# Moving the newest adds, an addition and the expert layers within a fused attention and mixture-of-depths kernel

## The chip, the cores and the metric

The kernel runs on one core of one Trainium2 chip. The metric is the device time of one execution in microseconds (us). Before the change the median of three runs was 548.92 us (548.64 to 553.21).

The engines are named as in the profile: PE is TensorE (matmuls), PEld its weight loads, DVE is VectorE, ACT is ScalarE, POOL is GpSimd, and SP is the queue from which most DMAs are issued. Each works through its own instructions in the order in which the program emits them, and waits where another engine has to deliver first.

## The reference

Eight batches of attention, 12 heads, 448 tokens, head size 64, with normalised queries and keys. Its output, brought to `x[8, 448, 768]`, goes into a mixture of depths: a gate scores each token, the best 128 of a batch pass through two layers (768 to 1024 to 768), and the rest are copied.

```python
def rmsnorm(x, g):
    rms = np.sqrt(np.mean(x * x, axis=-1, keepdims=True) + 1e-06)
    return x / rms * g
q_n, k_n = (rmsnorm(q, g_q), rmsnorm(k, g_k))
scores = scale * np.matmul(q_n, k_n.transpose(0, 1, 3, 2))
attn = np.exp(scores - max); attn = attn / (sum + 1e-09)
out = np.matmul(attn, v)            # -> x (B, S, 768)
...
scores = np.einsum('bsd,d->bs', x, w_gate)
out = x.copy()
for b in range(B):
    top_idx = np.argpartition(-scores[b], capacity)[:capacity]   # 128
    xe = x[b, top_idx]
    ye = np.maximum(xe @ w1, 0.0) @ w2
    g = 1.0 / (1.0 + np.exp(-scores[b, top_idx]))
    out[b, top_idx] = x[b, top_idx] + g[:, None] * ye
```

(The line with `max` and `sum` is shortened from the original's.)

## The kernel before, in words

All the work is in the function `fast`. The 96 heads are taken in 24 **groups** of four (three groups to a batch). A group has seven **units**, each of them 64 of the 448 keys for its four heads, so there are 168 units.

For a unit, `scores` (L276) makes scores with the keys on the partitions, and ScalarE their exponents `p` (L285), scaled by the keys' norms. `values` (L302) multiplies `p` with the values into two PSUM banks that collect over the seven units. `add_probs` (L315) adds the unit's `p` into `sum` on VectorE; the first unit of a group needs no add. After a group's last unit come the steps that `finish` queues as **tasks**: `sum_keys` (den, L337) lets TensorE sum `sum` over the keys; `invert_sums` (denT, L355, then rden, L357) transposes that and takes the reciprocal; `to_tokens` (x_ps, L369, then x, L371) transposes 128 columns of the output and multiplies with rden, twice per group; `last_tokens` is the second of them and puts `gate` (L395, four products) into the slots. With the batch's last group `spread` follows (L408 to L416), and as a task `ranks_of`: row_ps (L424), its copy score_rows (L428), `count` (cmp, L438), `annotate`, `select` (L465, POOL scatters the chosen rows to a DRAM tile) and `load_selected` (SP loads them back as xe).

`mixture` runs the layers on the 128 rows. It is a generator that is advanced piece by piece: six transposes of xe (L499, the first three into the bank moe_ps, the others into the shared bank aux as xeT_ps) with two copies to xeT (L504); w1 in four pieces (L523) with the ReLU (hT, L532) after every second; w2 in four pieces (L542), each half followed by the gated addition on VectorE (L551); then POOL scatters the rows to the output (L560).

Queries are normalised ahead: `squares` (L191, ScalarE), `sum_squares` (ss: reduction L197 and 1e-6 L198 on VectorE, power rinv L201 on POOL), the norms' way through DRAM (`rows_out`, `rows_in`), and `scale_q` (qT, L235), due four units before the group's first scores.

The order of all this is written out by the loop at the end of `fast`, which goes through **sections** of four units (numbered from 0 to 41, two units being a half). In a section it emits:

- two units' scores, the values of the two units before, the adds of those; then the same for the second half;
- opening 0: one task that is due (tasks are taken from the front two of the list);
- for each half: the slots of its two units (`run`: squares, ss, loads, scale_q, gate, count), a piece of a mixture, and another opening.

A section in which a mixture has no piece is called light here, one with w1 or w2 full. PSUM has four banks for scores, two for values, one (aux) for the tasks and one (moe) for the mixture; `spare` lets a task use the latter where no mixture does. A bank is written again only after its reader is done, so a task's matmul can wait for the reader of the task before.

After the last scores there are no more sections to fill: the last values, tasks and mixtures follow each other. This is called the tail.

Of the kernel before, what the change touches and what calls it, by code (L numbers as in the profile page):

```python
# [11 lines left out]
I32 = mybir.dt.int32  # L12
# [14 lines left out]
def fast(  # L27
# [45 lines left out]
    const = ctx.enter_context(tc.tile_pool(name="const", bufs=1))  # L73
    load_pool = ctx.enter_context(tc.tile_pool(name="load", bufs=2))
    norm_pool = ctx.enter_context(tc.tile_pool(name="norm", bufs=2))
    p_pool = ctx.enter_context(tc.tile_pool(name="p", bufs=7))
    x_pool = ctx.enter_context(tc.tile_pool(name="x", bufs=2))
    moe_pool = ctx.enter_context(tc.tile_pool(name="moe", bufs=1))
    dram_pool = ctx.enter_context(
# [9 lines left out]

    def aux(shape, name):  # L90

        if spare[0]:
            return ps_moe.tile(shape, F32, tag="moe", name=name)
        return ps_aux.tile(shape, F32, tag="aux", name=name)
# [100 lines left out]
    def sum_squares(n, i, sq):  # L195
        ss = sss.pop((n, i))
        nc.vector.tensor_reduce(out=ss, in_=sq, axis=AX.X, op=OP.add)  # L197
        nc.vector.tensor_scalar_add(out=ss, in0=ss, scalar1=1e-6)  # L198
        rinv = norm_pool.tile([128, 2, NI], F32, name="rinv", bufs=8)
        flat = "p h i -> p (h i)"  # L200
        nc.gpsimd.tensor_tensor(  # L201
            out=rinv.rearrange(flat),
            in0=ss.rearrange(flat),
            in1=neg_half.to_broadcast([128, 2 * NI]),
            op=OP.pow,
        )
        rinvs[n, i] = rinv
# [31 lines left out]
    def scale_q_early(n):  # L239

        rinv = rinvs.pop((n, 0))
        for c in range(2):
            ps = ps_sc.tile([128, 512], F32, name="sc")
            r = slice(D * c, D * (c + 1))
            for i in range(NI):
                for hh in range(2):
                    nc.tensor.matmul(
                        out=ps[D * hh : D * (hh + 1), D * i : D * (i + 1)],
                        lhsT=rinv[r, hh, i : i + 1].to_broadcast([D, D]),
                        rhs=ident[r, r],  # L250
                        start=True,
                        stop=True,
                    )
            t = qTs[n][:, c].rearrange("d (p i) -> d p i", i=NI)
            nc.vector.scalar_tensor_tensor(
                out=t,
                in0=t,
                scalar=gg,
                in1=ps[:, 0:S].rearrange("d (i p) -> d p i", i=NI),
                op0=OP.mult,  # L260
                op1=OP.mult,
            )
# [4 lines left out]

    def scores(u):
        n, i = divmod(u, NI)
        scs = [ps_sc.tile([128, 512], F32, name="sc") for _ in range(2)]  # L270
        for c in range(2):
            for k0 in (0, 32):
                for hh in range(2):
                    r = slice(D * hh, D * (hh + 1))
                    o = D * c + k0
                    nc.tensor.matmul(  # L276
                        out=scs[hh][o : o + 32, 0:S],
                        lhsT=kTs[n][r, c, D * i + k0 : D * i + k0 + 32],
                        rhs=qTs[n][r, c, :],
                        start=True,  # L280
                        stop=True,
                    )
        p = p_pool.tile([128, 2, S], F32, name="p")
        for hh in range(2):
            nc.scalar.activation(  # L285
                out=p[:, hh],
                in_=scs[hh][:, 0:S],
                func=AF.Exp,
                scale=rinvs[n, 1][:, hh, i : i + 1],
            )  # L290
        probs[u] = p
# [194 lines left out]
    def mixture(b):  # L486

        n = CAP
        xe = xes.pop(b)
        xeT = moe_pool.tile([128, NDC, 128], F32, name="xeT")  # L490
        half = NDC // 2
        for a in range(2):
            if a == 0:
                ps = ps_moe.tile([128, 512], F32, tag="moe", name="moe_ps")
            else:
                ps = aux([128, 512], "xeT_ps")
            for i in range(half):
                dc = half * a + i
                nc.tensor.transpose(  # L499
                    out=ps[:, 128 * i : 128 * i + n],  # L500
                    in_=xe[:n, 128 * dc : 128 * (dc + 1)],
                    identity=ident[:n, :n],
                )
            nc.scalar.copy(  # L504
                out=xeT[:, half * a : half * (a + 1), :n],
                in_=ps[:, : half * 128].rearrange("p (i t) -> p i t", t=128)[:, :, :n],
            )
        row = moe_pool.tile([128, 1], I32, name="row", bufs=2)
        nc.vector.tensor_copy(out=row[:n], in_=xe[:n, DM + 1 : DM + 2])
        yield False  # L510

        def bank():

            if PER * now[0] >= units + 2:
                return ps_sc.tile([128, 512], F32, name="sc")
            return ps_moe.tile([128, 512], F32, tag="moe", name="moe_ps")

        hT = moe_pool.tile([128, NFC, 128], F32, name="hT")
        for f0 in range(0, NFC, 4):
            ps = bank()  # L520
            for i in range(4):
                for dc in range(NDC):
                    nc.tensor.matmul(  # L523
                        out=ps[:, 128 * i : 128 * i + n],
                        lhsT=w1[:, dc, 128 * (f0 + i) : 128 * (f0 + i + 1)],
                        rhs=xeT[:, dc, :n],
                        start=(dc == 0),
                        stop=(dc == NDC - 1),
                    )
                if i == 1:  # L530
                    yield False
            nc.scalar.activation(  # L532
                out=hT[:, f0 : f0 + 4, :n],
                in_=ps.rearrange("p (i t) -> p i t", t=128)[:, :, :n],
                func=AF.Relu,
            )
            yield True
        for a in range(2):
            cols = slice(DM // 2 * a, DM // 2 * (a + 1))
            ps = bank()  # L540
            for fc in range(NFC):
                nc.tensor.matmul(  # L542
                    out=ps[:n, : DM // 2],
                    lhsT=hT[:, fc, :n],
                    rhs=w2[:, fc, cols],
                    start=(fc == 0),
                    stop=(fc == NFC - 1),
                )
                if fc == NFC // 2 - 1:
                    yield False  # L550
            nc.vector.scalar_tensor_tensor(  # L551
                out=xe[:n, cols],
                in0=ps[:n, : DM // 2],
                scalar=xe[:n, DM : DM + 1],
                in1=xe[:n, cols],
                op0=OP.mult,
                op1=OP.add,
            )
            if a == 1:
                nc.gpsimd.indirect_dma_start(  # L560
                    out=out.flatten_outer_dims(),
                    out_offset=bass.IndirectOffsetOnAxis(ap=row[:n, :1], axis=0),
                    in_=xe[:n, 0:DM],
                    in_offset=None,
                )
            yield True

# [47 lines left out]

    def finish(n, q):

        task((q, 1), sum_keys, n)  # L620
        task((q, 2), invert_sums, n)
        task((q + 1, 0), to_tokens, n, 0)
# [19 lines left out]
    def ranks_of(b):  # L642
# [3 lines left out]
        at(s + 1, count, b, (2, 3))  # L646
        at(s + 2, annotate, b)
        at(s + 2, select, b)
        at(s + 6 if s >= 0 else s + 3, load_selected, b)
        ready[b] = max((s + 6) // PER + 1, first_ff(b)) if b < B - 1 else 0  # L650

    def first_ff(b):


        return (units - NG * NI * (B - 2 - b)) // PER

    def run_values(upto, q):
        ended = False
        while waiting and waiting[0] <= upto:
            u = waiting[0]  # L660
            if ended and u % NI == 0:

                return
            values(waiting.pop(0))
            if u % NI == NI - 1:
                values_out(u // NI)
                finish(u // NI, q)
                ended = True
            add_probs(u)

    sq = {}
    for key in ((0, 0), (0, 1), (1, 0), (1, 1)):
# [12 lines left out]
                fn()  # L685

    def piece(q):
        nonlocal moe, done
        end = next(moe, None)
        if end is None and ready.get(done, q + 1) <= q:  # L690
            moe = mixture(done)
            done += 1
            next(moe)
            opening(q, 1)
            end = next(moe)
        return end

    waiting = list(range(units))
    moe, ready, done, q = iter(()), {}, 0, 0
    while done < B or tasks:  # L700
        now[:] = q, 0
        k = PER * q
        for half in range(HALVES):
            for u in (k + 2 * half, k + 2 * half + 1):
                if u < units:
                    scores(u)
            run_values(k + 2 * half - 1, q)
        opening(q, 0)
        for half in range(HALVES):
            run((k + 2 * half, k + 2 * half + 1))  # L710
            end = piece(q)
            spare[0] = end is None and half == 0
            if end is not None or half == 0 or not ready:
                opening(q, half + 1)
            spare[0] = False
            run(())
# [532 lines left out]
```

## Time and profile before

| | |
|---|---|
| median of the runs | 548.92 us |
| the profiled execution: time, span | 548.22 us, 546.5 us |
| TensorE busy | 507.3 us (93%) |
| VectorE busy | 356.1 us (65%) |
| ScalarE busy | 277.1 us (51%) |
| GpSimd busy | 188.2 us (34%) |
| granted TensorE clock | 0.991 |
| start of sections 3, 10, 13, 41 | 38.73, 98.56, 140.32, 474.94 us |
| end of the last matmul | 540.03 us |

The span is what the profile shows of one execution; 1.7 us of its time lie around it. A timeline line gives start and length in us, engine, line, operation, out<-in, the shape of out<-in and how many instructions are merged in it; brackets give how long the engine had stood idle and what released it. A section's start is that of its first scores on TensorE.

### The profile page before, as it was taken

What the parts mean: (1) busy time and instruction counts of PE and PEld (TensorE: products, weight loads), DVE (VectorE), ACT (ScalarE), POOL (GpSimd) and SP (SyncE); (2) the same over time, 40 slices, a digit from 0 to 9 for tenths busy, and PEclk for the clock granted to TensorE, in tenths of its full rate; (3) what the DMA queues carried; (4) which work ended last, traced back from release to release, by engine and by line L of the source; (5) the groups of instructions that cost most, each with busy time, mean ns of one, the idle gap of its engine ahead of it and who ended that gap; (6) DMA issues with size and microseconds to landing.
All of it is one profiled execution on the core that took longest, in us unless ns stands there. A gap on an engine that the chain in (4) does not pass through costs nothing.

```text
span 546.5 us, 16420 instructions
## 1 busy us (share of the span) xinstructions
PE 507.3 (93%) x7084; PEld 288.3 (53%) x7084; DVE 356.1 (65%) x700; ACT 277.1 (51%) x506; POOL 188.2 (34%) x100
## 2 busy tenths in 40 slices
PE   6999788899998999899998999989998999989795
PEld 6543343366446644366443764466443664457492
DVE  3687899866776577866877467855977735865100
ACT  3678667644464454655467255454638443531000
POOL 3763537341263233541342325422434210400300
PEclk9999999999999999999999899999999999999999
DMA  6975989895655537592837546445657123203200
GB/s 225 348 207 166 315 271 342 301 315 190 175 154 172 171 92 255 153 262 82 268 93 231 170 137 201 153 143 170 167 167 230 31 75 103 88 3 101 87 2 33
DMA packets 46532, 93.55 MB, mean 171 GB/s; under 512 B 11382, under 2 KB 29302, under 8 KB 46452
## 3 DMA queue, kind: packets, MB, share of 16 engines
q1 hardware_dynamic: 43108, 86.12, 50.6%
q0 software_dynamic: 3200, 6.31, 3.5%
q8 instruction: 57, 0.93, 0.7%
q14 instruction: 23, 0.19, 0.1%
q10 hardware_dynamic: 144, 0.00, 0.0%
HBM read 74.93 MB, written 25.35 MB: 184 GB/s over the span
## 4 chain that ended last, share of the span: by engine, by line
PE 55%; issue 19%; ACT 3%; DVE 2%; POOL 1%; DMA 1%; POOLq 0%; DVEq 0%
PE sc L276 15%; PE av L302 13%; PE moe_ps L523 11%; PE moe_ps L542 10%; PE x_ps L369 3%; PE den_ps L337 1%; DVE sum L315 1%; POOL selected L465 1%; ACT p L285 1%; DMA out_dram<-xe,row 1%; ACT xeT L504 1%; PE denT_ps L355 1%; DVE ss L197 1%; ACT sq L191 1%; ACT xT L325 1%
## 5 line engine op out<-in xcount | busy, mean ns | idle before, releaser
L285 ACT ACTIVATE p<-sc,rinv 128x448 f32<-128x448 f32 x336 | 186.1, 641 | 98.8 <-PE sc L276 83.7
L201 POOL TENSOR_TENSOR rinv<-ss,neg_half 128x14 f32<-128x14 f32 x48 | 140.0, 2919 | 221.0 <-DVE ss L198 120.4
L276 PE MATMUL sc<-qT,kT 64*32 64x448 f32 x2688 | 152.0, 540 | 7.1 <-issue 5.0
L302 PE MATMUL av<-p,v 64*32 64x448 f32 x2688 | 149.3, 536 | 0.0
L315 DVE TENSOR_TENSOR sum<-sum,p 128x896 f32<-128x896 f32 x120 | 130.5, 1088 | 9.4 <-ACT p L285 1.7
L302 PEld LDWEIGHTS av<-p,v 64*32 64x32 f32 x2688 | 55.4, 107 | 71.4 <-issue 64.3
L276 PEld LDWEIGHTS sc<-qT,kT 64*32 64x32 f32 x2688 | 49.0, 106 | 77.4 <-issue 51.7
L523 PE MATMUL moe_ps<-xeT,w 128*128 128x128 f32 x624 | 75.8, 280 | 0.0
L523 PEld LDWEIGHTS moe_ps<-xeT,w 128*128 128x128 f32 x624 | 73.1, 195 | 3.3 <-issue 3.3
L371 DVE TENSOR_TENSOR x<-x_ps,rden 112x512 f32<-112x512 f32 x48 | 33.1, 690 | 58.9 <-PE x_ps L369 57.4
L465 POOL DMA_INDIRECT selected<-x,rank x32 | 34.7, 1084 | 98.0 <-DVE x L457 90.3
L542 PE MATMUL moe_ps<-w,hT 128*128 128x384 f32 x192 | 66.4, 489 | 0.0
L197 DVE TENSOR_REDUCE ss<-sq 128x14 f32<-128x896 f32 x48 | 51.9, 1080 | 11.6 <-ACT sq L191 11.6
L191 ACT ACTIVATE sq<-tok 128x896 f32<-128x896 f32 x48 | 45.5, 965 | 4.7 <-DMA tok<-in_tok_dram 3.3
L542 PEld LDWEIGHTS moe_ps<-w,hT 128*128 128x128 f32 x192 | 34.6, 190 | 21.3 <-issue 2.2
L395 DVE SCALAR_TENSOR_TENSOR prod<-x,wg 112x256 f32<-112x256 f32 x96 | 40.9, 426 | 2.9
L532 ACT ACTIVATE hT<-moe_ps 128x512 f32<-128x512 f32 x13 | 7.8, 597 | 65.4 <-PE moe_ps L523 65.4
L369 PE MATMUL x_ps<-ident,xT 128*112 128x128 f32 x192 | 29.5, 278 | 5.4 <-ACT xeT L504 3.4
L357 DVE RECIPROCAL rden<-denT_ps 112x16 f32<-112x16 f32 x24 | 6.1, 254 | 40.8 <-PE denT_ps L355 40.8
L369 PEld LDWEIGHTS x_ps<-ident,xT 128*112 128x112 f32 x192 | 21.2, 134 | 20.3 <-issue 10.7
L438 DVE SCALAR_TENSOR_TENSOR cmp<-score_rows,gate,earlier 112x448 f32<-112x448 f32 x32 | 21.9, 684 | 10.6 <-ACT score_rows L428 9.9
L315 DVE TENSOR_TENSOR sum<-p 128x896 f32<-128x896 f32 x24 | 26.0, 1082 | 3.6 <-ACT p L285 3.6
(63 smaller groups left out, 280.8 us busy)
## 6 DMA issues: line engine op xcount, KB each, us to landing
tok<-in_tok_dram SPq DMA_DIRECT2D x48, 448.0 KB, 6.1
qT<-in_qT_dram SPq DMA_DIRECT2D x24, 448.0 KB, 5.9
kT<-in_kT_dram SPq DMA_DIRECT2D x24, 448.0 KB, 5.6
v<-in_vp_dram SPq DMA_DIRECT2D x24, 448.0 KB, 7.0
out_dram<-x SPq DMA_DIRECT2D x8, 1344.0 KB, 7.6
bc<-rows SPq DMA_DIRECT2D x44, 224.0 KB, 5.3
xe<-selected SPq DMA_DIRECT2D x8, 385.0 KB, 3.1
w<-in_moe_w_dram SPq DMA_DIRECT2D x6, 512.0 KB, 8.1
```

The source lines that it names most:

```text
L191: nc.scalar.activation(out=sq, in_=t, func=AF.Square, scale=scale)
L197: nc.vector.tensor_reduce(out=ss, in_=sq, axis=AX.X, op=OP.add)
L201: nc.gpsimd.tensor_tensor(out=rinv.rearrange(flat), in0=ss.rearrange(flat), in1=neg_half.to_broadcast([128, 2 * NI]), op=OP.pow,)
L276: nc.tensor.matmul(out=scs[hh][o : o + 32, 0:S], lhsT=kTs[n][r, c, D * i + k0 : D * i + k0 + 32], rhs=qTs[n][r, c, :], start=True, stop=True,)
L285: nc.scalar.activation(out=p[:, hh], in_=scs[hh][:, 0:S], func=AF.Exp, scale=rinvs[n, 1][:, hh, i : i + 1],)
L302: nc.tensor.matmul(out=avs[n][c][o : o + 32, 0:S], lhsT=vs[n][r, hh, i, d0 : d0 + 32], rhs=probs[u][r, hh], start=(i == 0), stop=(i == NI ...
L315: nc.vector.tensor_tensor(out=sums[n], in0=probs[u - 1] if i == 1 else sums[n], in1=probs[u], op=OP.add)
L369: nc.tensor.transpose(out=ps[:CP, j, :], in_=t[:, j, :], identity=ident)
L395: nc.vector.scalar_tensor_tensor(out=prod, in0=xs[b][:, j, cols], scalar=1.0, in1=wg[:, cols], op0=OP.mult, op1=OP.mult, accum_out=gates[b ...
L465: w = nc.gpsimd.indirect_dma_start(out=t[:, :], out_offset=bass.IndirectOffsetOnAxis(ap=rank[:, j : j + 1], axis=0), in_=x[:, j, :], in_of ...
L523: nc.tensor.matmul(out=ps[:, 128 * i : 128 * i + n], lhsT=w1[:, dc, 128 * (f0 + i) : 128 * (f0 + i + 1)], rhs=xeT[:, dc, :n], start=(dc == 0),
L542: nc.tensor.matmul(out=ps[:n, : DM // 2], lhsT=hT[:, fc, :n], rhs=w2[:, fc, cols], start=(fc == 0), stop=(fc == NFC - 1),)
```

## The change

- `sum_squares`: the addition of 1e-6 is made by GpSimd instead of VectorE.
- The loop: the adds of the units whose values were emitted in a half come later, those of the first half behind the second half's scores, those of the second half behind opening 0. `p` has eight buffers instead of seven.
- `mixture`: each half of the transposes is a piece of its own, both go through the bank moe, and w1 begins in the next piece, so in the following section. `piece` only says whether a piece was emitted. The last opening of a section is used where a piece was emitted in its second half or more than two tasks wait.
- The selected rows are loaded two slots earlier, and `ready` and `first_ff`, which say when a mixture may begin, are changed with it: the first begins in section 12 instead of 10, the following in 17, 22, 28, 33 and 38 instead of 15, 21, 26, 31 and 36.
- The tail: all tasks of the last group are due at once, and from the last scores on the tasks and mixtures take the scores' four banks.

```diff
-    p_pool = ctx.enter_context(tc.tile_pool(name="p", bufs=7))
+    p_pool = ctx.enter_context(tc.tile_pool(name="p", bufs=8))
...
     def aux(shape, name):
+        if PER * now[0] >= units:
+            return ps_sc.tile(shape, F32, tag="sc", name=name)
...
-        nc.vector.tensor_scalar_add(out=ss, in0=ss, scalar1=1e-6)
+        nc.gpsimd.tensor_scalar_add(ss, ss, 1e-6)
...
+        def bank():
+            if PER * now[0] >= units:
+                return ps_sc.tile([128, 512], F32, tag="sc", name="sc")
+            return ps_moe.tile([128, 512], F32, tag="moe", name="moe_ps")
+
         for a in range(2):
-            if a == 0:
-                ps = ps_moe.tile([128, 512], F32, tag="moe", name="moe_ps")
-            else:
-                ps = aux([128, 512], "xeT_ps")
+            ps = bank()
...
-        yield False
...
+            if a == 1:
+                row = moe_pool.tile([128, 1], I32, name="row", bufs=2)
+                nc.vector.tensor_copy(out=row[:n], in_=xe[:n, DM + 1 : DM + 2])
+            yield
...
     def finish(n, q):
+        if n == n_groups - 1:
+            for fn, args in ((sum_keys, (n,)), (invert_sums, (n,)), (to_tokens, (n, 0))):
+                task((q, 1), fn, *args)
+            task((q, 1), last_tokens, n)
+            return
...
-        at(s + 6 if s >= 0 else s + 3, load_selected, b)
-        ready[b] = max((s + 6) // PER + 1, first_ff(b)) if b < B - 1 else 0
+        at(s + 4 if s >= 0 else s + 3, load_selected, b)
+        ready[b] = max((s + 4) // PER + 1, first_ff(b) - 1) if b < B - 1 else 0
...
-        return (units - NG * NI * (B - 2 - b)) // PER
+        return -(-(units + 2 * PER - NG * NI * (B - 2 - b)) // PER)
...
     def run_values(upto, q):
-        ended = False
+        done, ended = [], False
...
-            add_probs(u)
+        return done
...
     def piece(q):
         nonlocal moe, done
-        end = next(moe, None)
-        if end is None and ready.get(done, q + 1) <= q:
-            moe = mixture(done)
-            done += 1
-            next(moe)
-            opening(q, 1)
-            end = next(moe)
-        return end
+        if next(moe, moe) is not moe:
+            return True
+        if ready.get(done, q + 1) > q:
+            return False
+        moe = mixture(done)
+        done += 1
+        next(moe)
+        return True
...
+        late = []
         for half in range(HALVES):
             for u in (k + 2 * half, k + 2 * half + 1):
                 if u < units:
                     scores(u)
-            run_values(k + 2 * half - 1, q)
+            for u in late:
+                add_probs(u)
+            late = run_values(k + 2 * half - 1, q)
         opening(q, 0)
+        for u in late:
+            add_probs(u)
         for half in range(HALVES):
             run((k + 2 * half, k + 2 * half + 1))
-            end = piece(q)
-            spare[0] = end is None and half == 0
-            if end is not None or half == 0 or not ready:
+            some = piece(q)
+            spare[0] = not some and half == 0
+            if some or half == 0 or len(tasks) > 2:
                 opening(q, half + 1)
```

## The prediction

> **What bounds the kernel now.** I read the engines' shares first, then the pauses of TensorE in order of time, then what VectorE does around them. The page's first part:
>
> ```profile
> span 546.5 us, 16420 instructions
> ...
> PE 507.3 (93%) x7084; PEld 288.3 (53%) x7084; DVE 356.1 (65%) x700; ACT 277.1 (51%) x506; POOL 188.2 (34%) x100
> ```
>
> TensorE has work for 507.3 us. The change adds it none, so the forecast is about the other 39.2 us. The timeline of TensorE places them: 5.1 before the first matmul, 6.5 after the last, 8.9 at the transposes of the six earlier mixtures, 6.7 in the tail (after the scores end), 11.5 at the sections without layer work. The mean of 65% for VectorE hides that these last are VectorE's. Busy time by stretch (columns: window, its length, then each engine's busy time):
>
> ```profile
> 38.73:98.56 59.83, 52.38 (x971) 22.48 (x971) 51.51 (x95) 42.52 (x77) 31.82 (x18) 1.00 0.85 279
> 115.85:153.64 37.79, 37.79 (x500) 20.87 (x496) 25.93 (x52) 18.75 (x35) 11.68 (x6) 1.00 0.64 198
> ```
>
> The first window is sections 3 to 9 (no layers): VectorE is busy 51.5 of 59.8 us, and a section takes 8.5 us though TensorE has 7.5 for it. The second is sections 11 to 13 (with layers): TensorE never stops and VectorE has a third of its time free. Anything that makes VectorE wait costs in light sections and is hidden in full ones. This is how a light section runs (VectorE's timeline, then TensorE's):
>
> ```profile
> 39.01 4.62 DVE L315 TENSOR_TENSOR sum<-sum,p 128x896 f32<-128x896 f32 x4
> 45.59 0.69 DVE L371 TENSOR_TENSOR x<-x_ps,rden 112x512 f32<-112x512 f32 x1 [1.96 <-PE x_ps L369]
> ```
>
> ```profile
> 44.90 1.08 PE L369 MATMUL x_ps<-ident,xT 128*112 128x128 f32 x8
> 46.34 0.59 PE L337 MATMUL den_ps<-sum,pick_pair 128*32 128x224 f32 x8 [0.35 <-DVE x L371]
> ```
>
> All four adds (1.155 us each) end at 43.63. VectorE then waits for x_ps, which TensorE can only make after scores and values, 6.2 us into the section. den, which reads the finished sum, is held just 0.35 us, by the bank and not by the sum.
>
> **The change, part by part.**
>
> *Newest adds behind the first opening.* VectorE works in the order written. The two newest of four adds now stand behind the multiply (or reciprocal) of the first opening, so they cannot start before TensorE has made x_ps, though their data lies there 3 us earlier. Behind them on VectorE stand the slots' work (ss, scale_q), the second x and the gate. Three things wait for these.
>
> First, den. In section 3 the multiply would end at 46.2, two adds at 48.5, and den starts there instead of 46.34: +2.2. Second, scale_q, which the scores of a new group need in the next section:
>
> ```profile
> 68.77 3.49 DVE L315 TENSOR_TENSOR sum<-sum,p 128x896 f32<-128x896 f32 x3
> 72.55 0.69 DVE L371 TENSOR_TENSOR x<-x_ps,rden 112x512 f32<-112x512 f32 x1 [0.30 <-PE x_ps L369]
> 73.16 1.14 DVE L235 SCALAR_TENSOR_TENSOR qT<-qT,gg,bc 128x896 f32<-128x896 f32 x1
> ```
>
> ```profile
> 74.41 1.74 PE L276 MATMUL sc<-qT,kT 64*32 64x448 f32 x32 [1.45 <-issue]
> ```
>
> The scores at 74.41 waited 1.45 us, with the reason given as "issue", and start as scale_q ends. With two adds (2.3) between multiply and scale_q the wait is about 3.7. Third, the gate, spread and so row_ps.
>
> On the other side a reciprocal or multiply no longer waits for two adds: the 1.68 us ahead of the second x in section 4 goes.
>
> I carried this through sections 3 to 12, engine by engine in the new instruction order, with these durations: score or value block 1.5, x or den 0.58, add 1.155, multiply 0.7, scale_q 1.1, ss 1.1, gate 1.9. Against the same sections of before without their layer work (15.9 us: 48 w1 at 2.68 per 24, 16 w2 at 2.58 per 8 and again 48 w1), in us: section 3 +2.4 (den); 4 -2.3; 5 +3.0 (unit 21 waits 2.5 for scale_q, then den 2.0 where it waited 1.9); 6 +2.1; 7 +1.4; 8 -0.3; 9 +1.1; 10 and 11 -0.9 together; 12 +7.0 (unit 49 waits 2.5 for scale_q, den 1.5, row_ps 3 for the gate). Sum +13.5. Section 12 is the least sure, since three waits in a row are assumed there with nothing caught up; I take 5 of its 7: **+11.5**. From below the term could be 0: if VectorE is so far behind that x_ps always lies ready when it gets there, the order costs nothing. From above 15.
>
> *Layers one section later.* The first mixture starts in section 12 instead of 10, so three more sections are light; that is in the sum above. Later each mixture leaves one section with transposes alone, some 8 us long, and these behave as light ones. In 17 and 38 the order is x, transposes, x, transposes, den: the second x waits 0.4 for the bank, the second transposes 0.8 for ScalarE (xT 0.98, sq 0.96 and xeT 0.49 stand in its queue), and den 2.2 because the second multiply stands behind two adds and ss: 3.5 each. 22: 0.4. 28: 1.5. 33: 2.7 (second transposes behind xT and sq). The scores of group 16 now follow a light section (27) and wait 3.7. Sum 15.3.
>
> *Selected rows' transposes split.* What goes is seen at any mixture of before:
>
> ```profile
> 168.22 0.55 PE L499 MATMUL xeT_ps<-ident,xe 128*128 128x128 f32 x3 [0.94 <-DVE row L509]
> 169.33 0.65 PE L369 MATMUL x_ps<-ident,xT 128*112 128x128 f32 x4 [0.57 <-ACT xeT L504]
> ```
>
> The shared aux bank cost 0.94 and 0.57 here. The excess of these sections over their matmuls was 1.5, 1.2, 3.9, 1.4 and 1.5 (sections 15, 21, 26, 31, 36), and the scores of group 12, which followed a light section (2.40 at 230.91) now follow one with w2: 11.9 go. With 15.3 that come: **+3.4**, from -4 (the new sections cost as little as 22) to +7.
>
> *The tail.* The last scores' sections now leave half of mixture 5's w2 for it, and w1 of mixture 6 comes behind row_ps instead of ahead. What goes:
>
> ```profile
> 501.30 0.57 PE L424 MATMUL row_ps<-ident,spread 112*112 112x112 f32 x4 [0.70 <-DVE parts L416]
> ...
> 516.29 0.70 PE L499 MATMUL moe_ps<-ident,xe 128*128 128x128 f32 x3 [4.09 <-DMA xe<-selected]
> ```
>
> From row_ps to the arrival of the last rows are 15.0 us, covered before by 10.5 of w2, afterwards by 12.1 + 10.5: the 4.09 go. What comes: between the last x_ps and row_ps lie multiply, gate and spread (497.92 to 501.30, 3.4 us), covered before by 24 w1 matmuls, now by three transposes: a pause of 3.2 instead of 0.70. With 1.0 and 0.6 gone at the transposes: **-2.4**, from -5 to 0. After the 4.09 pause three transposes took 0.70 instead of 0.49, and granted clock was 0.97 in this window against 1.00. [...]
>
> *1e-6 on GpSimd.* 48 VectorE instructions of 0.176 go (8.5 us, counted above as ss 1.1 instead of 1.28). No row shows such an add on GpSimd. Below stands the 128x1 memset at 0.1, above the power on the same tile, 2.92. I take 0.2, near the 128x128 select (0.29), as it has 14 elements a partition. GpSimd is idle 65%, and rinv is made two sections ahead, so 0. At 2.9 it would cost the start: the power block from 9.88 to 20.14 gates the first exponents. [...]
>
> *Queues.* SP's load of the selected rows moves one load forward twice, POOL's scatters keep their order among the powers, and the eighth p buffer lets the later-released probabilities live: 0.
>
> **Sum**: 548.2 (profiled execution; span 546.5 and 1.7 around it) + 11.5 + 3.4 - 2.4 = **561**. The runs' median, 548.92, is 0.7 above the profiled one; a comparison of this kernel cannot tell less than 1% (5.5 us) from nothing.
>
> **Rivals.** *Half of it* (0.2): VectorE's lateness overlaps, so that a wait for scale_q removes the wait for den behind it; half of 11.5 and no net in the later sections: 552. For it: sections 4 and 8 already gain. *The gains alone* (0.13), the other side: in light sections VectorE enters with a backlog. Does it reach 4.6 us at a section's start, the multiply is reached only as x_ps is ready, and the reordering costs nothing. Then 5.9 of the 8.9 us at the transposes, the 2.4 in the tail: 540. For it: at 55.27 and 91.98 the reciprocal came 1.8 and 1.5 us after its matmul. Against: the 1.96 us of idle shown above, which would be 4 with two adds fewer ahead of it. *GpSimd's add at the price of a power* (0.04): the first rinv 2.9 later, the fourth 11: some 8 at the start that nothing hides: 569 with the rest. That the change doesn't do what it says I leave out: the instruction order of each engine shows all parts.
>
> **Numbers.** 561 has 0.63. Range 548 to 568: it leaves out most of the gains' case and the worst of mine and of GpSimd's. Slower by over 1% 0.75, within 1% 0.14, faster 0.11.
>
> **What would show it.** Right: den in section 3 waits 2 us for sum; scores of unit 21, 28 and 49 wait 2.5 to 4 us as scale_q ends; VectorE idle ahead of the first multiply in light sections, adds right behind it; no xe wait in the tail and 3 us ahead of row_ps. Wrong: sections 3 to 12 as short as before, or the first exponents later than 16.7 us.

## The result and the profile after

| | before | changed |
|---|---|---|
| median of six runs each | 550.21 us | 577.24 us |
| profiled execution: time, span | 548.22, 546.5 us | 578.25, 576.2 us |
| TensorE busy | 507.3 us | 523.7 us |
| span less TensorE busy | 39.2 us | 52.5 us |
| granted TensorE clock | 0.991 | 0.962 |

The ratio of changed to before is 1.047 (95% interval 1.041 to 1.052): slower by 27 us, where 12.5 had been forecast. The ratios here and below are estimated from the fast runs (slow ones, among them one of 763 us in a later experiment, are left out), so they differ a little from the quotient of two medians (1.049 here). The span grew by 29.7 us. Of these 13.3 are new pauses of TensorE, and 16.4 are more busy time for the very same 7084 matmuls. The page of the changed kernel (engine's busy time; granted clock in 40 slices):

```profile
span 576.2 us, 16447 instructions
...
PE 523.7 (91%) x7084; PEld 292.5 (51%) x7084; DVE 344.0 (60%) x652; ACT 279.0 (48%) x506; POOL 220.0 (38%) x148
...
PEclk9998989989899989999999979999999989997998
```

An 8 or 7 in the last line is a slice in which the array was for a part at half its clock (0.5 in its clock record). The clock record in the trace has nine such stretches between the start and the last matmul, six of 3.41 us and three of 6.83, 41.0 us in all; the kernel before has two, 6.8 us in all. Half of the difference is 17 us, which is about the 16.4.

Section 3 shows both parts. VectorE's timeline of the changed kernel (start, length, instruction, idle time before):

```profile
39.63 2.23 DVE L317 TENSOR_TENSOR sum<-sum,p 128x896 f32<-128x896 f32 x2
46.21 0.69 DVE L373 TENSOR_TENSOR x<-x_ps,rden 112x512 f32<-112x512 f32 x1 [4.35 <-PE x_ps L371]
46.82 2.28 DVE L317 TENSOR_TENSOR sum<-sum,p 128x896 f32<-128x896 f32 x2
```

Only two adds stand ahead of the multiply now. VectorE idles 4.35 us for x_ps (1.96 before) and makes the two newest adds after it. TensorE's timeline of the same stretch:

```profile
45.52 1.09 PE L371 MATMUL x_ps<-ident,xT 128*112 128x128 f32 x8
49.24 0.59 PE L339 MATMUL den_ps<-sum,pick_pair 128*32 128x224 f32 x8 [2.63 <-DVE sum L317]
49.75 2.52 PE L278 MATMUL sc<-qT,kT 64*32 64x448 f32 x32
51.98 2.71 PE L304 MATMUL av<-p,v 64*32 64x448 f32 x32
54.48 1.71 PE L278 MATMUL sc<-qT,kT 64*32 64x448 f32 x32
```

den waits 2.63 us, now for the sum (0.35 before, for the bank). And then something follows that no wait explains: the next scores and values take 2.52 and 2.71 us where 1.7 is usual, from which they recover at 54.48. No engine holds them up; the array is at half clock from 50.56 to 53.98 by the clock record. The step from section 6 to 7, VectorE and then TensorE:

```profile
80.04 0.69 DVE L373 TENSOR_TENSOR x<-x_ps,rden 112x512 f32<-112x512 f32 x1 [4.86 <-PE x_ps L371]
80.65 2.27 DVE L317 TENSOR_TENSOR sum<-sum,p 128x896 f32<-128x896 f32 x2
82.84 1.15 DVE L237 SCALAR_TENSOR_TENSOR qT<-qT,gg,bc 128x896 f32<-128x896 f32 x1
```

```profile
84.08 2.73 PE L278 MATMUL sc<-qT,kT 64*32 64x448 f32 x32 [3.65 <-issue]
86.45 2.57 PE L304 MATMUL av<-p,v 64*32 64x448 f32 x32
```

The two adds stand between the multiply and scale_q, the new group's scores wait 3.65 us (1.45 before), and again the two blocks behind run slow. By stretch, sections 3 to 9 and 10 to 13 of the changed kernel (window, length, busy times, then granted clock):

```profile
39.31:111.39 72.08, 57.94 (x973) 24.41 (x972) 52.29 (x97) 43.48 (x78) 36.24 (x25) 0.93 0.74 233
111.39:162.17 50.78, 40.90 (x616) 20.18 (x614) 33.71 (x65) 26.77 (x48) 18.54 (x10) 0.90 0.80 240
```

Sections 3 to 9 took 59.83 us before and 72.08 now: 6.7 us more of pauses and 5.6 more of busy time at a clock of 0.93. In sections 10 to 13, of which the first three have no w1 or w2 now, it is 0.90. The tail, TensorE's timeline:

```profile
522.61 0.96 PE L426 MATMUL row_ps<-ident,spread 112*112 112x112 f32 x4 [3.11 <-DVE parts L418]
523.37 13.31 PE L524 MATMUL sc<-xeT,w 128*128 128x128 f32 x96
...
547.95 10.98 PE L524 MATMUL sc<-xeT,w 128*128 128x128 f32 x96 [0.29 <-ACT xeT L510]
```

The 4.09 us wait for the last rows is gone: mixture 7 follows with 0.29. Ahead of row_ps stands the new pause of 3.11, and w1 behind it takes 13.31 us; w1 of mixture 7, further on, took 10.98.

### The profile page after: what moved, and what is told of

Read it like the earlier page. It is cut to its first block, busy times and chain, and to the rows that moved or that the text cites. A ratio compares the mean times of both kernels' runs of the same rounds, so it can differ in the third digit from the quotient of the medians.

```text
span 576.2 us, 16447 instructions
## 1 busy us (share of the span) xinstructions
PE 523.7 (91%) x7084; PEld 292.5 (51%) x7084; DVE 344.0 (60%) x652; ACT 279.0 (48%) x506; POOL 220.0 (38%) x148
## 5 line engine op out<-in xcount | busy, mean ns | idle before, releaser
L278 PE MATMUL sc<-qT,kT 64*32 64x448 f32 x2688 | 160.9, 571 | 12.7 <-issue 10.1
L304 PE MATMUL av<-p,v 64*32 64x448 f32 x2688 | 154.3, 554 | 0.0
L200 POOL TENSOR_SCALAR ss<-ss 128x14 f32<-128x14 f32 x48 | 25.3, 527 | 192.6 <-DVE ss L199 167.8
L524 PE MATMUL moe_ps<-xeT,w 128*128 128x128 f32 x576 | 69.2, 277 | 0.0
L524 PEld LDWEIGHTS moe_ps<-xeT,w 128*128 128x128 f32 x576 | 66.2, 192 | 4.3 <-issue 4.3
L467 POOL DMA_INDIRECT selected<-x,rank x32 | 38.6, 1205 | 67.2 <-DVE x L459 58.5
L543 PE MATMUL moe_ps<-w,hT 128*128 128x384 f32 x176 | 61.2, 491 | 0.0
L561 POOL DMA_INDIRECT out_dram<-xe,row x8 | 12.3, 1542 | 82.9 <-DVE rden L359 37.7
L543 PEld LDWEIGHTS moe_ps<-w,hT 128*128 128x128 f32 x176 | 31.7, 190 | 21.8 <-issue 2.9
L552 DVE SCALAR_TENSOR_TENSOR xe<-sc,xe 128x384 f32<-128x384 f32 x5 | 3.1, 617 | 44.5 <-PE sc L543 44.5
```

Of the source, the lines that this page charges most:

```text
L278: nc.tensor.matmul(out=scs[hh][o : o + 32, 0:S], lhsT=kTs[n][r, c, D * i + k0 : D * i + k0 + 32], rhs=qTs[n][r, c, :], start=True, stop=True,)
L304: nc.tensor.matmul(out=avs[n][c][o : o + 32, 0:S], lhsT=vs[n][r, hh, i, d0 : d0 + 32], rhs=probs[u][r, hh], start=(i == 0), stop=(i == NI ...
L467: w = nc.gpsimd.indirect_dma_start(out=t[:, :], out_offset=bass.IndirectOffsetOnAxis(ap=rank[:, j : j + 1], axis=0), in_=x[:, j, :], in_of ...
L524: nc.tensor.matmul(out=ps[:, 128 * i : 128 * i + n], lhsT=w1[:, dc, 128 * (f0 + i) : 128 * (f0 + i + 1)], rhs=xeT[:, dc, :n], start=(dc == 0),
L543: nc.tensor.matmul(out=ps[:n, : DM // 2], lhsT=hT[:, fc, :n], rhs=w2[:, fc, cols], start=(fc == 0), stop=(fc == NFC - 1),)
```

## Experiments

The runs fall into three sets, each with the kernel before beside it. It took 564.1 us in the first set (the first four experiments), 551.7 in the second (the late adds in full sections, the tail alone and the two with old adds that follow) and 566.9 in the third (the changed kernel and the one with filled pauses again, and the last experiment). So ratios to the kernel before of the same set are compared, not times.

### The adds back in their old place

```diff
             values(waiting.pop(0))
-            done.append(u)
...
                 ended = True
+            add_probs(u)
```

> The changed kernel with every add back where it stood (directly behind its unit's values); all else of the change stays. Theory A (the late adds make TensorE pause, and after each long pause it runs some 3.4 us at half clock): the waits of 2.6 to 3.7 us at den and at a new group's scores shrink by two adds (2.3 us) each, the half-clock stretches go, granted clock back to 0.98 to 0.99; about 552 us (548 to 557). Rival B (the layers one section later, with three more light sections and five sections of transposes alone, are what costs): 565 or more.

Measured: ratio 0.990 (0.987 to 0.994), 559.66 us, clock 0.984. Everything else of the change stays, and the kernel is about 1% faster than before; the expected 552 would have been 1.006 of the 548.92 it started from. Section 3 of it, TensorE:

```profile
47.19 0.58 PE L339 MATMUL den_ps<-sum,pick_pair 128*32 128x224 f32 x8 [0.35 <-DVE x L373]
47.71 1.74 PE L278 MATMUL sc<-qT,kT 64*32 64x448 f32 x32
49.24 1.71 PE L304 MATMUL av<-p,v 64*32 64x448 f32 x32
```

den waits for the bank again, and scores and values run at full speed. Rival B falls. Three half-clock stretches are left: at den of section 5 (2.24 us of pause), at row_ps of section 12 (pauses of 0.46, 0.99 and 1.34 close together) and at that of the tail.

### The late adds alone

```diff
# the kernel before, with
+        late = []
         for half in range(HALVES):
...
-            run_values(k + 2 * half - 1, q)
+            for u in late:
+                add_probs(u)
+            late = run_values(k + 2 * half - 1, q)
         opening(q, 0)
+        for u in late:
+            add_probs(u)
```

> The kernel before with the newest adds behind the first opening as the only change (and the eighth p buffer they need). Theory A: den in section 3 and the scores of units 21, 28 and 84 wait 2.3 us longer, some four to five half-clock stretches of 1.7 us loss each are added; about 565 us (558 to 572). Rival B: within 1% of before (545 to 555).

Measured: ratio 1.041 (1.037 to 1.046), 588.76 us where before took 564.14; the expected 565 was 1.03 of the 549 it started from. One part of the change makes nearly all of its loss. Section 7 of it:

```profile
84.20 2.57 PE L276 MATMUL sc<-qT,kT 64*32 64x448 f32 x32 [3.65 <-issue]
86.41 2.72 PE L302 MATMUL av<-p,v 64*32 64x448 f32 x32
```

The same 3.65 and the same slow blocks as in the changed kernel. The clock record has ten half-clock stretches (granted clock 0.969), eight more than before, where four to five had been expected.

### 1e-6 on VectorE again

```diff
-        nc.gpsimd.tensor_scalar_add(ss, ss, 1e-6)
+        nc.vector.tensor_scalar_add(out=ss, in0=ss, scalar1=1e-6)
```

> The changed kernel with 1e-6 on VectorE again. The GpSimd instruction measured 0.53 us and moved the first scores by 0.8 us; on VectorE 0.17 us for each of 48 comes back. Theory A: 577 within 3 us (0.8 gained at the start, up to 2 lost in the light sections). Rival C (GpSimd's extra 25 us of work delay rinv or hinder VectorE): 570 or less.

Measured: ratio 1.040 (1.034 to 1.045), against 1.047 (1.041 to 1.052) and, in the third set, 1.031 (1.024 to 1.038) for the changed kernel. No difference can be told: 1.040 lies between the two forecasts (1.046 to 1.057, and 1.038 or less, as ratios to 548.92) and decides for neither. The 0.8 us at the start, with which the expectation reckoned, were not the addition's. The block of 60 warming transposes took 8.92 us instead of 8.13, which makes the first scores later; with the late adds alone, and the addition on VectorE, it took 9.05. What the addition costs on GpSimd (line, count, shortest, median and longest in ns):

```profile
L200 POOL TENSOR_SCALAR ss<-ss x48: 259/363/1090, 9.7 to 452.0; 128x14 f32<-128x14 f32 x48
```

### The pauses filled

```diff
+    fill_sc = {21: 22, 28: 30, 49: 18, 112: 30}
+    fill_den = {1: 20, 2: 14, 5: 20, 6: 12, 9: 2}
+    fill_row = {1: 18, 7: 24}
+
+    def fill(ps, count):
+        for _ in range(count):
+            nc.tensor.transpose(out=ps[:, 0:128], in_=ident, identity=ident)
...
+        fill(scs[0], fill_sc.get(u, 0))     # in scores
+        fill(ps, fill_den.get(n, 0))        # in sum_keys
+        fill(ps, fill_row.get(b, 0))        # in score_rows
```

> The changed kernel with dummy transposes of the identity (228 in all, each some 0.13 us, written to banks that the waiting matmuls overwrite) put ahead of the matmuls that wait longest: scores of units 21, 28, 49, 112, den of groups 1, 2, 5, 6, 9, row_ps of batches 1 and 7. The waits themselves stay, only TensorE isn't idle in them. Theory A (clock): the half-clock stretches behind them go, clock 0.98 or more, time falls by 9 to 15 us to 562 to 568, though nothing is taken out and work is added. Rival D (the longer TensorE time has another cause than the clock after pauses): 577 or more.

Measured: ratio 1.020 (1.014 to 1.026), clock 0.986, in another set than the changed kernel's first run. So both were run again beside each other:

> The changed kernel itself, beside the one with filled pauses on the same chip: ratio to before 1.04 to 1.055.

> The changed kernel with 228 dummy transposes in its longest pauses, on the same chip as the changed kernel. Theory A (clock): 2 to 3.5% faster than the changed kernel, ratio to before 1.01 to 1.025. If the earlier difference came from the two chips: within 1% of the changed kernel.

Measured: the changed kernel 583.42 us, ratio 1.031 (1.024 to 1.038), less than expected; with filled pauses 572.86 us, ratio 1.014 (1.007 to 1.021). 10.6 us less (1.8%, a little under the 2 to 3.5 expected), though VectorE's work and the waits are the same and 210 more matmuls are in the records (of the 228, some are missing there). The first 111 us from section 3 on, the changed kernel, then the filled one:

```profile
39.00:150.00 111.00, 88.69 (x1434) 36.62 (x1442) 79.16 (x143) 66.14 (x121) 54.68 (x35) 0.91 0.78 241
```

```profile
39.00:150.00 111.00, 106.34 (x1722) 56.05 (x1707) 82.08 (x148) 69.15 (x125) 52.92 (x35) 1.00 0.84 258
```

The clock goes from 0.91 to 1.00, and VectorE gets through more in the same time. Where the changed kernel idled 3.65 us ahead of section 7, the filled one has:

```profile
76.06 3.44 PE L276 MATMUL sc<-ident 128*128 128x128 f32 x30
79.83 1.74 PE L287 MATMUL sc<-qT,kT 64*32 64x448 f32 x32 [0.33 <-DVE qT L237]
81.36 1.72 PE L313 MATMUL av<-p,v 64*32 64x448 f32 x32
```

The scores still start only as scale_q ends (the releaser is named now), but they and the values take 1.7 us. That the clock is what makes the blocks behind a pause slow is shown by this: nothing but idleness was taken away. The clock record keeps two half-clock stretches (10.2 us) of the ten (41.0 us), and over the whole execution the granted clock is 0.989 instead of 0.961.

### Late adds in full sections only

```diff
+        if q not in full:                   # sections without w1 or w2
+            for u in late:
+                add_probs(u)
+            late = []
         opening(q, 0)
         for u in late:
             add_probs(u)
```

> The changed kernel with the newest adds behind the first opening only in the 23 sections that hold w1 or w2, and ahead of it in all others. Theory A says that the wait of VectorE for the first opening costs only where TensorE has no layer work to go on with: ratio to before 0.98 to 1.00, the same as with all adds in the old place (0.990) within 0.6%. Rival E (the late adds also cost in full sections): 1.01 or more.

Measured: ratio 0.998 (0.993 to 1.003), 550.61 us. That is in the range of Theory A, but 0.8% above the 0.990, where 0.6% had been allowed. Beside the kernel with old adds of the same set (0.9945, 548.62 us, two experiments below), which differs in the place of 1e-6 too, no cost of the late adds in full sections can be told; one of some 2 us can't be excluded. The profile has no half-clock stretch before the last matmul (granted clock 0.996). The loss of 4% belongs to the sections without w1 or w2.

### The tail alone

```diff
# the kernel before, with the changed finish() for the last group, and
+        if PER * now[0] >= units:
+            return ps_sc.tile(shape, F32, tag="sc", name=name)
...
-            if PER * now[0] >= units + 2:
+            if PER * now[0] >= units:
```

> The kernel before with the tail's part alone (all tasks of the last group due at once, the scores' banks for tasks and mixtures once the scores have ended); layers, transposes, adds and 1e-6 as before. The pauses of 1.01, 0.57 and 0.70 us go, the wait of about 4 us for the last selected rows stays, since only w2 of mixture 6 lies behind row_ps: some 2 us, ratio 0.993 to 1.000. If the wait for the rows goes too, 0.985 to 0.993.

Measured: ratio 0.998 (0.995 to 1.001). As expected for the wait that stays (4.36 us in the profile), but not to be told from nothing.

### All but the late adds and GpSimd's addition

The first experiment with the diff of the third.

> The changed kernel with the adds in the old place and 1e-6 on VectorE: the rest of the change alone (layers one section later, split transposes, tail). The start is 0.8 us earlier than with GpSimd's add, the light sections lose up to 0.2 us each: ratio 0.985 to 0.995. If GpSimd's add was a gain in the light sections: 0.995 or more.

Measured: ratio 0.9945 (0.991 to 0.998), 548.62 us. Beside the first experiment's 0.990 (0.987 to 0.994) in another set, no effect of the place of the addition can be told. The rest of the change brings some 3 us (1 to 5 by the interval).

### The same with three pauses filled

```diff
+    fill_den = {2: 16}
+    fill_row = {1: 9, 7: 22}
```

> As the kernel before it (old adds, 1e-6 on VectorE), with 47 dummy transposes of the identity in the three pauses that were followed by half clock with old adds: den of group 2, row_ps of batch 1 and of batch 7. By the clock theory 3 to 5 us less than without them (0.5 to 0.9%), no half-clock stretch between the start and the end: ratio 0.977 to 0.988. Without the clock's part in it: equal or slower than without them.

Measured: ratio 0.990 (0.987 to 0.994), 547.23 us; 1.4 us under the one before it, less than the 3 to 5 expected, and the intervals overlap; two half-clock stretches are left (granted clock 0.990) where none was expected. A part of the reason is seen in the row_ps of the tail, in the first experiment and then in the kernel without fills:

```profile
505.04 0.95 PE L426 MATMUL row_ps<-ident,spread 112*112 112x112 f32 x4 [3.11 <-DVE parts L418]
```

```profile
496.28 0.57 PE L426 MATMUL row_ps<-ident,spread 112*112 112x112 f32 x4 [3.11 <-DVE parts L418]
```

The same pause of 3.11 us, and in one execution the clock fell (0.95), in the other it didn't (0.57). There was less to save than the expectation had taken from one profile; why the clock fell once and not the other time is not shown.

### row_ps behind a part of w1

```diff
# the last but one, and
-        tasks.insert(0, ((q, 2) if place == 0 else (q + 1, place - 1), lambda: ranks_of(b)))
+        when = (q, 2) if place == 0 else (q + 1, place - (b < B - 1))
+        tasks.insert(0, (when, lambda: ranks_of(b)))
...
+    fill_den = {2: 16}
+    fill_row = {1: 9}
```

> Adds in the old place, 1e-6 on VectorE, and row_ps of the last batch behind a quarter of w1 of mixture 6 instead of ahead of all of it; dummy transposes only at den of group 2 and row_ps of batch 1. The pause of 3.1 us ahead of the last row_ps becomes some 0.4 us and the last rows still come in time (15 us after row_ps, with 9.4 + 10.5 us of layers behind it): 2.7 us less than 0.9945, with the fills ratio 0.980 to 0.989. If the rows come late the gain is eaten by a wait for xe: 0.990 or more.

Measured: ratio 0.977 (0.970 to 0.984), 552.76 us beside 566.89 of before. It is faster than the kernel before and the changed one (583.42 in the same set), and a little better than expected. The tail:

```profile
499.56 3.01 PE L535 MATMUL sc<-xeT,w 128*128 128x128 f32 x24
502.75 0.59 PE L437 MATMUL row_ps<-ident,spread 112*112 112x112 f32 x4 [0.18 <-DVE spread L423]
503.18 8.22 PE L535 MATMUL sc<-xeT,w 128*128 128x128 f32 x72
```

Real work fills the pause: 3.11 us became 0.18, and w1 runs at full speed. The pause accounts for some 3 us. The gain, 13 us and at least 9 by the interval, is somewhat more than this and the 5 us of the version before (0.990 in another set) together; what makes up the rest is not settled.

## Why the prediction was wrong

The direction was right, the size was not: 577 lies above the range of 548 to 568. The step that failed is that the sum counts a pause as its own length and no more: it has no term for the clock behind the pauses, which measured 16.4 us, more than all the terms in the sum together. The prediction held the very row that should have priced it: after the pause of 4.09 us three transposes took 0.70 instead of 0.49. The upper end of the range took no account of it either. The longest pauses alone would not have been enough: the three of 3.11 to 3.65 us at 1.7 each, an estimate (half of a half-clock stretch of 3.41), make 5 us, or 566, while the clock fell nine times, six of them behind pauses of 1.78 to 2.63 us. The kernel before had shown that too, in section 26:

```profile
300.67 0.59 PE L337 MATMUL den_ps<-sum,pick_pair 128*32 128x224 f32 x8 [1.40 <-ACT xeT L504]
301.18 7.25 PE L523 MATMUL moe_ps<-xeT,w 128*128 128x128 f32 x48
```

After pauses of 0.46 and 1.40 us, 48 w1 matmuls took 7.25 us instead of 5.6. The clock record has a half-clock stretch there (301.5 to 304.9). The prediction counted the section's 3.9 us as waits; 1.9 were.

The pauses themselves, step by step:

| wait | forecast, us | measured, us |
|---|---|---|
| den, section 3 | +2.2 | 2.63 (0.35 before) |
| scores of unit 21 | 2.5 | 2.76 |
| den, section 5 | 2.0 | 1.78 |
| scores of unit 28 (section 7) | 3.7 | 3.65 |
| scores of unit 49, den and row_ps in section 12 | 2.5, 1.5, 3 | 2.25, 1.55, 2.30 |
| second x, second transposes, den in section 17 | 0.4, 0.8, 2.2 | 0.46, 0.38, 2.22 |
| scores of group 16 (section 28) | 3.7 | 3.65 |
| den, section 10 | none named | 2.63 |
| x_ps, section 13 | none named | 1.16 |
| sections 28, 33 and 38, new pauses in all | 1.5, 2.7, 3.5 | 1.02, 1.85, 2.27 |
| row_ps in the tail | 3.2 | 3.11 |
| pauses in all, against before | +12.5 | +13.3 |

The rows show the waits themselves where no plus stands. That the last line fits to 1 us is partly luck: sections 3 to 12 gave +12.7 (13.5 worked out, 11.5 booked), the tail -3.3 instead of -2.4.

- *Newest adds.* Right in mechanism, place and pauses; the first two experiments show it from both sides (0.990 without, 1.041 with them alone). Of the 2.3 us that section 4 was to gain 0.6 came: the 1.68 went, but the section started at half clock and took 8.67 us instead of 9.30.
- *Layers one section later.* In the changed kernel 12.3 us of pauses came (15.3 forecast) and 9.9 went (11.9 forecast). With the adds in the old place 7.3 of the 12.3 are left in the profile, and one of 1.46 is new, so there the part saves pauses, about 1 us. So the +3.4 (2.4 came) was the late adds' share, booked under the layers. No run has this part alone; all of the change but the late adds gains 0.5 to 1%.
- *Tail.* The xe wait went and the pause at row_ps came, both to 0.1 us. The terms written there add up to -3.2 and not to -2.4; pauses from section 41 on shrank by 3.3 us. What the sum left out is the clock behind the 3.11.
- *1e-6 on GpSimd.* 0.2 was taken, 0.36 is the median and 0.53 the mean. No cost in the kernel's time can be told, as said.
- *Rivals.* "Half of it" took the waits to overlap; they did not. "The gains alone" needed VectorE to come late to the first multiply; it idled 4.35 and 4.86 us ahead of it. GpSimd's price was refuted by its row.
- *The clock behind a pause.* In section 3 of the changed kernel the clock was back after 3.41 us (50.56 to 53.98). It fell behind single pauses of 2.63 us (den at 49.24) and even 1.82 (den at 469.61), in the first experiment behind one of 2.24 (den at 64.62), but not behind the 2.76 us ahead of the changed kernel's scores at 62.16. Behind the 3.11 us ahead of the last row_ps it fell in the changed kernel and in the first experiment (row_ps took 0.96 and 0.95), in the kernel without fills it did not (0.57).
- *What stood ahead of the falls.* In the clock records of the kernel before and of the changed one, all 24 distances from one change of the clock to the next are whole multiples of 3.413 us (to 0.001). Cut into pieces of this length at these changes, the two traces show how much of a piece TensorE was busy (by its records, whose ends are modelled). It was 7 to 47% of the piece ahead of each of the 11 falls up to the last matmul, and 51% or more of each of the 295 other pieces at full clock. At half clock, it was 83% or more of the 11 pieces that ended in full clock, and 54, 68 and 70% of the three that did not: these make the stretches of 6.83 us. The pause of 2.76 us lay across two pieces, busy to 59 and 60%. So in these two traces it is not the length of one pause that went with a fall but the idle share of the 3.413 us ahead of it.

## What to carry to other kernels

An instruction that is ready should not be put behind one that waits for another engine, on an engine that makes its instructions in the order written, as VectorE did here (it idled 4.35 us ahead of the multiply in section 3, with two adds behind it), and that has little time to spare in that stretch: price the move by what then idles, stretch by stretch, not by the engine's mean share. Where the trace shows slow matmuls behind pauses of the array, count the pauses twice: once for themselves and once for these matmuls (here 13.3 and 16.4 us). Where a pause can't be avoided, real work moved into it is best (here 3.11 us of pause became 0.18), and even empty matmuls can pay (here 10.6 us).

## What the runs showed that was not expected

- Half-clock stretches came in lengths of 3.41 or 6.83 us in the changed kernel, and a pause of 1.82 us there, or three of 0.46, 0.99 and 1.34 close together in the first experiment, sufficed for one.
- Adding over two hundred matmuls without use made a kernel 1.8% faster.
- The kernel before took 550 to 567 us in different sets of runs, 564 and 552 in two that the record puts on the same chip. No run here shows the reason. In the first experiment's profile a block of values took 4.09 us where 1.71 is usual, at full clock (1.00 from 270.31 to 285.93) and with no release shown. What stops it stays open.
